# An attention tile's product with the carried state: q scaled ahead by GpSimd, and the sum made in one bank

## The chip, the cores and the metric

The kernel runs on one core of a Trainium2 chip. The metric is the device time of one execution in microseconds (us). PE is TensorE, DVE is VectorE, ACT is ScalarE, POOL is GpSimd and SP is the engine that issues the DMAs.

## The reference

Three stages follow each other. The first is an mLSTM attention with 2 batches, 8 heads, 768 steps and heads of 40; the second and third are two MoE layers (1536 tokens, width 320).

```python
for t in range(S):
    kt, vt, qt = (k[:, :, t], v[:, :, t], q[:, :, t])
    m_new = np.maximum(f_gate[:, :, t] + m, i_gate[:, :, t])
    f_stab = np.exp(f_gate[:, :, t] + m - m_new)
    i_stab = np.exp(i_gate[:, :, t] - m_new)
    m = m_new
    C = f_stab[:, :, None, None] * C + i_stab[:, :, None, None] * np.einsum('bhd,bhe->bhde', vt, kt)
    n = f_stab[:, :, None] * n + i_stab[:, :, None] * kt
    h_tilde = np.einsum('bhde,bhe->bhd', C, qt)
    nq = np.einsum('bhd,bhd->bh', n, qt)[:, :, None]
    denom = np.maximum(np.abs(nq), 1.0)
    o = 1.0 / (1.0 + np.exp(-o_gate[:, :, t]))
    y[:, :, t] = o * h_tilde / denom
```

Then `x = y`, `g(x @ w_in) @ w_out` with a piecewise g, and a second MoE of 8 experts whose gate weights are normalized eight times.

## The kernel before

**Attention.** The sequence is cut into chunks of 128 steps, and a tile is one chunk of one batch: 12 tiles, t = 2 * chunk + batch. Within a tile the recurrence is written as a masked product. `scores` (L434) multiplies keys by queries for four heads at a time into a bank of tag "at"; `scan` (L419) turns the gates f of the chunk, broadcast over the partitions by `load_g` (L171) into G0 or G1, into a triangle of decays on DVE; `gated` (L448) multiplies the scores by it into A; `values` (L425) and `keys` (L461) scale v and k on POOL; `values_sum` (L471) sums A by v in a bank "at". What earlier chunks left is the state `Cst`, one for each batch, 104 partitions by 4 pairs of heads by 82 columns: 40 rows and 41 columns for each head, two heads on the diagonal of a pair (the 41st column is n). `attn` (L523) multiplies q by the state into the bank "ax" (L540 to L542), scales the product by the decay since the chunk's start, which `gt` holds for each token in its columns 16 to 31 (L554), and adds the weighted sum to it (L558); both go through the tile `hv` on DVE. `gate_out` (L503) divides by the denominator and multiplies by the sigmoid into `sg`, `turn` (L513) transposes that into a bank "ax", and `split_x` (L140) writes it as two parts XH and XL. The state is multiplied by the whole chunk's decay on POOL (L550), `update` (L484) makes the new chunk's part in a bank "at", and `add_update` (L493) adds it to the state on DVE, in two instructions for the two heads of a pair (for the first chunk ACT copies it).

**Gates.** Before the tiles, `gate_max`, `gate_exps` and `gate_prods` (L363 to L393) make the gates in the rows g_f, g_i and g_m; g_m then holds the running products of f in each chunk. `gate_prods` writes g_f to DRAM (`g_d`), from where `load_g` broadcasts it. `gate_by_token` (L395) transposes g_i and g_m by 16 rows on PE into `gt`.

**Order.** Tiles 0 and 1 and the preparation of the first weights are written out by hand in one order (to L664, where `ordered` is cleared). From there tiles 2 to 11 are a generator of steps (`attn_rest`, L575), and the loop over the blocks of the first MoE (L787) takes `nf * RATE[si]` steps of it for each block (L838). Stage 0 makes the first half of the hidden units for tokens 0 to 511 in 8 blocks, stage 1 for tokens 512 to 1023 in 8 blocks; after stage 1 the rest of the attention is taken. In this part the framework's scheduler sets the order of each engine from its own estimate of the times, with the program's order as priority; each engine then runs its queue in order. PSUM banks come from `bank` (L94): two of tag "g1" for the MoE's first product, one each of "g2a", "g2b" and "g2c", two of "at", one of "ax". SP's DMAs (load_g, load_qk, load_kvo, and the loads of weight pieces) are one queue in order. The first tiles have warming matmuls (`warm`, L352) in the bank of the weighted sum.

The second MoE (from L1061) follows when the first is done.

Of the kernel before, what the change touches and what calls it, by code (L numbers as in the profile page):

```python
# [7 lines left out]
F32 = mybir.dt.float32  # L8
# [6 lines left out]
ALU = mybir.AluOpType  # L15
# [3 lines left out]
L = 128  # L19
# [15 lines left out]
WA, WG, WF = 4, 2, 12  # L35
RATE = (3.1, 4.5, 0, 0, 0)

# [6 lines left out]
def mlstm_moe_moe_kernel(  # L44
# [109 lines left out]
    with ExitStack() as atx:  # L154
# [10 lines left out]
        dram = ctx.enter_context(tc.tile_pool(name="dram", bufs=1, space=bass.MemoryType.DRAM))  # L165
        g_d = dram.tile([16, S - L], F32, name="g_d")
        nc.sync.dma_start(g_f, gates[:, S : 2 * S])
# [3 lines left out]
        def load_g(t):  # L171
            c, b = divmod(t, 2)
            nc.sync.dma_start(
                G1 if t % 2 else G0, g_d[b * 8 : b * 8 + 8, (c - 1) * L : c * L].unsqueeze(0).to_broadcast([128, 8, L])
            )

        def load_qk(t):
# [26 lines left out]
        for a in QK:  # L204
            vec.memset(a[32:64, 0:2], 0.0)
            vec.memset(a[64:128, 1], 0.0)
            gp.memset(a[0:64, 2], 0.0)


# [133 lines left out]
        lend = ap.tile([104, NCH * 8], F32, name="lend")  # L343
        gt = ap.tile([128, NCH, 32], F32, name="gt")
        Cst = ap.tile([104, B, 4, 82], F32, name="Cst")
# [30 lines left out]
        def gate_prods(c0, c1):  # L376
            if c0 == 0:
                act(out=g_s, in_=g_f[:, 0:L], func=ACTF.Copy)
            for c in range(c0, c1):
                cs = slice(c * L, (c + 1) * L)  # L380
                vec.tensor_tensor_scan(out=g_m[:, cs], data0=g_f[:, cs], data1=zer, initial=1.0, op0=ALU.mult, op1=ALU.add)
            if c0 == 0:
                vec.scalar_tensor_tensor(
                    out=g_s, in0=f(g_s), scalar=cst[0:32, C_N16 : C_N16 + 1], in1=g_f[:, 0:L], op0=ALU.mult, op1=ALU.add,
                )
                vec.tensor_copy(g_s[:, 0:1], zer[:, 0:1])
            else:
                gp.tensor_copy(
                    g_f[:, c0 * L : c1 * L].rearrange("p (c t) -> p c t", t=L)[:, :, 0:1], zer[:, 0 : c1 - c0].unsqueeze(2)
                )  # L390
                for j in range(4):
                    o = j // 2 * 8 + j % 2
                    nc.sync.dma_start(g_d[j * 4 : j * 4 + 4, :], g_f[o : o + 7 : 2, L:S])  # L393

        def gate_by_token(c0, c1):  # L395
            p = bank("g1")
            for c in range(c0, c1):
                cs = slice(c * L, (c + 1) * L)
                o = (c - c0) * 32
                transpose(p[:, o : o + 16], g_i[0:16, cs], ident[0:16, 0:16])  # L400
                transpose(p[:, o + 16 : o + 32], g_m[0:16, cs], ident[0:16, 0:16])
            act(out=gt[:, c0:c1, :], in_=p[:, 0 : 32 * (c1 - c0)].rearrange("p (c e) -> p c e", e=32), func=ACTF.Copy)

# [12 lines left out]

        scanned = set()

# [51 lines left out]

        def values_sum(A, vw, tag, n):  # L471
            pa = bank(tag)
            if n:
                warm(n, pa)
            for h in range(8):
                mm(pa[:, h * 41 : (h + 1) * 41], A[h % 2][:, h // 2, :], vw[:, h, :], start=True, stop=True)
            return pa
# [15 lines left out]
        def add_update(t, pu):  # L493
            c, b = divmod(t, 2)
            puv = pu[0:104, 0:328].rearrange("p (r d) -> p r d", r=4)
            for par in range(2):
                rs, es = slice(par * 64, par * 64 + 40), slice(par * 41, par * 41 + 41)
                if c:
                    vec.tensor_tensor(out=Cst[rs, b, :, es], in0=puv[rs, :, es], in1=Cst[rs, b, :, es], op=ALU.add)
                else:  # L500
                    act(out=Cst[rs, b, :, es], in_=puv[rs, :, es], func=ACTF.Copy)
# [18 lines left out]
        def heads(p):  # L520
            return p[:, 0:328].rearrange("p (h d) -> p h d", h=8)

        def attn(t):  # L523
            c, b = divmod(t, 2)
            last = c == NCH - 1
            if t not in scanned:
                scan(t)
            vw = values(t)
            yield
# [8 lines left out]
            if t + 2 < NTILE:  # L538
                load_g(t + 2)
            pi = bank("ax")  # L540
            for pr in range(4):
                mm(pi[:, pr * 82 : (pr + 1) * 82], tiles_in[t][0][0:104, 0, pr, :], Cst[:, b, pr, :], start=True, stop=True)  # L542
            pa = values_sum(A, vw, "at", WA if t < 5 else 0)
            if t + 1 < NTILE:
                scan(t + 1)
            sg = sigmoid(t)
            yield
            if not last:
# [4 lines left out]
                )  # L553
            hv = ap.tile([128, 8, 41], F32, name="hv", tag="hv")  # L554
            vec.tensor_tensor(
                out=hv, in0=heads(pi), in1=gt[:, c, 16 + b * 8 : 16 + b * 8 + 8].unsqueeze(2).to_broadcast([128, 8, 41]), op=ALU.mult,
            )
            vec.tensor_tensor(out=hv, in0=hv, in1=heads(pa), op=ALU.add)  # L558
            gate_out(hv, sg)
            yield  # L560
# [95 lines left out]
        for t in (2, 3):  # L656
            load_g(t)
        piece(2)
        piece(1)
# [622 lines left out]
```

## Time and profile before

| | us |
|---|---|
| median of 3 runs | 955.72 |
| lowest, highest | 955.15, 961.31 |
| the profiled execution's own time | 955.23 |
| its span, from first to last instruction | 952.2 |

The profile is of one execution, so sums are made against its own time. An engine's busy time counts its instructions; matmuls are pipelined, and the records show each until it has drained. Where a helper on line 69 records the operations, the names of the tiles tell them apart: `bk_at` is a bank of tag "at", and out<-in stands for what is written from what. A number in brackets is the idle time of the engine before the instruction and what released it.

### The profile page before, as it was taken

Reading aid. Unit: us, or ns where it says so; the run is one execution under the profiler, and the core shown is the slowest. Engines: PE = TensorE matmul, PEld = TensorE weight load, DVE = VectorE, ACT = ScalarE, POOL = GpSimd, SP = SyncE. Lnnn points to the kernel's source line nnn. Section 1 sums busy time; section 2 is a strip of 40 time slices with the busy share of each in tenths; the row PEclk is TensorE's granted clock in tenths of the full one; section 3 lists DMA queues with packets and bytes.
Section 4 is the critical chain, followed back from the end, with each engine's and each line's share of the span. In section 5 each row is a group of like instructions: output and inputs, shape, how many; then the busy total and the mean of one; then the engine's idle time right before and its main releaser. Section 6 shows DMA issues by size and latency. Waiting matters only on the chain.

```text
span 952.2 us, 14707 instructions
## 1 busy us (share of the span) xinstructions
PE 938.7 (99%) x5696; PEld 879.9 (92%) x5702; DVE 664.6 (70%) x1122; ACT 428.6 (45%) x766; POOL 310.3 (33%) x364
## 2 busy tenths in 40 slices
PE   9899999999999999999999999999999999999998
PEld 6689988878878899999999999999999999999998
DVE  8898884764553656767857866775786687678565
ACT  4764565978754333534414523432442443343211
POOL 3222210000017567674505612450461254144000
PEclk9999999999999999999999999999999999999999
DMA  8684530130011101201200210220120021010011
GB/s 250 197 229 138 171 113 2 34 116 2 1 45 40 34 5 45 67 23 59 73 15 23 73 50 1 62 78 6 30 87 28 8 84 55 1 48 26 1 43 42
DMA packets 36437, 57.22 MB, mean 60 GB/s; under 512 B 2976, under 2 KB 26400, under 8 KB 36368
## 3 DMA queue, kind: packets, MB, share of 16 engines
q1 hardware_dynamic: 36368, 56.29, 19.9%
q8 instruction: 44, 0.72, 0.3%
q14 instruction: 25, 0.20, 0.1%
HBM read 52.70 MB, written 2.01 MB: 57 GB/s over the span
## 4 chain that ended last, share of the span: by engine, by line
PE 89%; DVE 7%; ACT 2%; issue 1%; POOL 1%; DVEq 0%; POOLq 0%
PE bk_g L69 41%; PE bk_at L69 17%; PE bk_ax L69 9%; PE bk_g2c L69 8%; PE bk_g2a L69 7%; PE bk_g2b L69 7%; DVE g_all L69 1%; DVE G L69 1%; DVE raw L69 0%; DVE sg L69 0%; DVE wf L69 0%; DVE den L69 0%; DVE scr L69 0%; DVE wk L69 0%; DVE hv L69 0%
## 5 line engine op out<-in xcount | busy, mean ns | idle before, releaser
L69 ACT ACTIVATE hi<-t 128x768 fp32r<-128x768 f32 x112 | 94.8, 847 | 346.3 <-DVE t L69 346.3
L69 PE MATMUL bk_g<-XH,wk 128*128 128x512 f32 (+2 forms) x638 | 199.7, 365 | 2.3 <-DVE t L69 1.7
L69 DVE TENSOR_TENSOR t<-bk_g,t 128x384 f32<-128x384 f32 x224 | 124.4, 555 | 78.5 <-PE bk_g L69 76.6
L69 PE MATMUL bk_g<-XL,wk 128*128 128x512 f32 (+2 forms) x394 | 141.6, 360 | 0.0
L69 DVE SCALAR_TENSOR_TENSOR lo<-t,hi 128x768 fp32r<-128x768 f32 x112 | 117.1, 1045 | 29.1 <-ACT hi L69 29.1
L69 PEld LDWEIGHTS bk_g<-XH,wk 128*128 128x128 f32 x638 | 117.7, 188 | 17.2 <-DVE t L69 2.0
L960 POOL TENSOR_TENSOR cb<-cb 128x256 f32<-128x256 f32 (+1 forms) x136 | 103.1, 776 | 49.0 <-DMA cb<-in_w1q_dram 20.2
L69 PE MATMUL bk_at<-wf,hi 128*128 128x320 f32 x448 | 101.0, 308 | 0.0
L1101 POOL TENSOR_TENSOR acc<-acc,ev 128x320 f32<-128x320 f32 x36 | 43.4, 1236 | 154.8 <-ACT ev L69 154.7
L69 PEld LDWEIGHTS bk_g<-XL,wk 128*128 128x128 f32 x394 | 74.3, 189 | 6.9
L69 DVE TENSOR_TENSOR t<-bk_g,u 128x384 f32<-128x384 f32 x112 | 61.5, 549 | 25.1 <-PE bk_g L69 24.4
L69 PEld LDWEIGHTS bk_at<-wf,hi 128*128 128x128 f32 x448 | 78.2, 188 | 0.0
L69 PE MATMUL bk_g<-XH,wf 128*128 128x384 f32 x238 | 73.9, 339 | 0.0
L69 PE MATMUL bk_g2b<-wf,hi 128*128 128x320 f32 x272 | 70.8, 309 | 0.0
L69 PE MATMUL bk_ax<-wf,hi 128*128 128x320 f32 x272 | 70.6, 308 | 0.0
L69 PE MATMUL bk_at<-wf,lo 128*128 128x320 f32 x224 | 68.7, 307 | 0.0
L69 PE MATMUL bk_g2c<-wf,hi 128*128 128x320 f32 x272 | 62.0, 308 | 0.0
L69 PE MATMUL bk_g2a<-wf,hi 128*128 128x320 f32 x272 | 61.9, 308 | 0.0
L69 ACT ACTIVATE gs<-gs 128x512 f32<-128x512 f32 x96 | 60.4, 629 | 1.9
L967 POOL TENSOR_TENSOR wf<-cb,wf 64x256 fp32r<-64x256 f32 (+2 forms) x35 | 38.3, 1102 | 55.4 <-ACT wf L69 31.5
L69 DVE TENSOR_TENSOR gs<-bk_g,gs 128x512 f32<-128x512 f32 x40 | 27.6, 689 | 36.8 <-ACT gs L69 36.6
L1015 POOL TENSOR_TENSOR t<-XH,XL 128x384 f32<-128x384 f32 x3 | 3.0, 1011 | 153.0 <-DVE XL L69 153.0
(285 smaller groups left out, 2156.1 us busy)
## 6 DMA issues: line engine op xcount, KB each, us to landing
cb<-in_w1q_dram SPq DMA_DIRECT2D x28, 512.0 KB, 4.5
raw<-in_w_dram SPq DMA_DIRECT2D x32, 320.0 KB, 3.1
kvo_t<-in_kvo_dram SPq DMA_DIRECT2D x12, 484.0 KB, 4.1
raw<-in_w_out_dram SPq DMA_DIRECT2D x8, 639.5 KB, 10.0
raw<-in_w_in_dram SPq DMA_DIRECT2D x8, 511.8 KB, 7.0
qk<-in_qk_dram SPq DMA_DIRECT2D x24, 160.0 KB
G<-g_d SPq DMA_DIRECT2D x5, 512.0 KB, 4.3
g_all<-g_d SPq DMA_DIRECT2D x5, 512.0 KB, 3.6
```

Source lines behind the costliest of these rows:

```text
L69: r = fn(*args, **kw)
L960: gp.tensor_tensor(out=c[:, o], in0=c[:, x], in1=c[:, y], op=op)
L967: gp.tensor_tensor(out=u[64:128, :, 2], in0=x[64:128, :, 1], in1=f(u[64:128, :, 2]), op=ALU.subtract)
L1015: gp.tensor_tensor(out=c[:, o : o + 2], in0=f(xh[:, k]), in1=f(xl[:, k]), op=ALU.add)
L1101: gp.tensor_tensor(out=acc[:, t, :], in0=acc[:, t, :], in1=ev, op=ALU.add)
```

## The change

`dq` is a new tile: the decay of each step of the chunk, broadcast by DMA over the 40 rows of a head, which POOL multiplies by q in place. The product of dq and the state is summed in the bank of the weighted sum, so `hv` is gone and `gate_out` reads the bank. The decays go to DRAM from g_m (`d_d`), like g_f. `add_update` copies the bank to SBUF with ACT, and POOL adds. RATE for stage 1 goes from 4.5 to 5. The transposes of g_m for `gt` are gone. The rest of the diff is the two DQ buffers, their memsets, and `load_d(2)` and `load_d(3)` behind `load_g` of the same tiles.

```diff
-RATE = (3.1, 4.5, 0, 0, 0)
+RATE = (3.1, 5, 0, 0, 0)
...
+        def load_d(t):
+            c, b = divmod(t, 2)
+            for r in range(2):
+                nc.sync.dma_start(
+                    DQ[t % 2][r * 64 : r * 64 + 40],
+                    d_d[b * 8 + r * 4 : b * 8 + r * 4 + 4, (c - 1) * L : c * L].unsqueeze(0).to_broadcast([40, 4, L]),
+                )
...
+        DQ = [ap.tile([128, 4, 128], F32, name=f"dq{i}", tag=f"dq{i}", bufs=1) for i in range(2)]
+        for a in DQ:
+            gp.memset(a[32:64], 0.0)
...
+                for j in range(4):
+                    o = j // 2 * 8 + j % 2
+                    nc.sync.dma_start(d_d[j * 4 : j * 4 + 4, :], g_m[o : o + 7 : 2, L:S])
...
-                transpose(p[:, o + 16 : o + 32], g_m[0:16, cs], ident[0:16, 0:16])
...
+        def decayed(t):
+
+            dq = DQ[t % 2][0:104]
+            gp.tensor_tensor(out=dq, in0=dq, in1=tiles_in[t][0][0:104, 0], op=ALU.mult)
+            return dq
+
-        def values_sum(A, vw, tag, n):
+        def values_sum(A, vw, tag, n, state=None):
             pa = bank(tag)
             if n:
                 warm(n, pa)
+            if state is not None:
+                dq, b = state
+                for pr in range(4):
+                    mm(pa[:, pr * 82 : (pr + 1) * 82], dq[:, pr, :], Cst[:, b, pr, :], start=pr == 0, stop=False)
             for h in range(8):
-                mm(pa[:, h * 41 : (h + 1) * 41], A[h % 2][:, h // 2, :], vw[:, h, :], start=True, stop=True)
+                mm(pa[:, h * 41 : (h + 1) * 41], A[h % 2][:, h // 2, :], vw[:, h, :], start=state is None, stop=state is None or h == 7)
             return pa
...
             c, b = divmod(t, 2)
+            if c:
+                ue = ap.tile([104, 328], F32, name="ue", tag="ue")
+                act(out=ue, in_=pu[0:104, 0:328], func=ACTF.Copy)
+                pu = ue
             puv = pu[0:104, 0:328].rearrange("p (r d) -> p r d", r=4)
...
                 if c:
-                    vec.tensor_tensor(out=Cst[rs, b, :, es], in0=puv[rs, :, es], in1=Cst[rs, b, :, es], op=ALU.add)
+                    gp.tensor_tensor(out=Cst[rs, b, :, es], in0=puv[rs, :, es], in1=Cst[rs, b, :, es], op=ALU.add)
...
+            if t not in dqs:
+                dqs[t] = decayed(t)
             vw = values(t)
...
-            pi = bank("ax")
-            for pr in range(4):
-                mm(pi[:, pr * 82 : (pr + 1) * 82], tiles_in[t][0][0:104, 0, pr, :], Cst[:, b, pr, :], start=True, stop=True)
-            pa = values_sum(A, vw, "at", WA if t < 5 else 0)
+            pa = values_sum(A, vw, "at", WA if t < 5 else 0, (dqs.pop(t), b))
+            if t + 2 < NTILE:
+                load_d(t + 2)
             if t + 1 < NTILE:
                 scan(t + 1)
+                dqs[t + 1] = decayed(t + 1)
...
-            hv = ap.tile([128, 8, 41], F32, name="hv", tag="hv")
-            vec.tensor_tensor(
-                out=hv, in0=heads(pi), in1=gt[:, c, 16 + b * 8 : 16 + b * 8 + 8].unsqueeze(2).to_broadcast([128, 8, 41]), op=ALU.mult,
-            )
-            vec.tensor_tensor(out=hv, in0=hv, in1=heads(pa), op=ALU.add)
-            gate_out(hv, sg)
+            gate_out(heads(pa), sg)
```

## Rows read from the trace of the kernel before

**Rows 1.** The page's busy time of each engine, with its share and instructions.

```profile
PE 938.7 (99%) x5696; PEld 879.9 (92%) x5702; DVE 664.6 (70%) x1122; ACT 428.6 (45%) x766; POOL 310.3 (33%) x364
```

**Rows 2.** Busy time by stretches: PE, PEld, DVE, ACT, POOL, clock, DMA share, GB/s.

```profile
25.00:50.00 25.00, 21.77 (x158) 18.14 (x160) 20.29 (x32) 18.96 (x36) 6.41 (x8) 1.00 0.63 203
...
45.00:135.00 90.00, 86.20 (x665) 78.77 (x668) 80.67 (x150) 50.98 (x95) 21.82 (x25) 1.00 0.59 173
135.00:280.00 145.00, 145.00 (x662) 117.65 (x661) 81.18 (x134) 105.77 (x192) 0.00 (x0) 1.00 0.09 25
```

**Rows 3.** The chain of waits from 82 to 94 us, shares by line.

```profile
by line: DVE G L69 19.4%; issue 14.6%; DVE g_all L69 14.6%; DVE hv L69 11.6%; DVE A L69 9.9%; DVE sg L69 5.2%; DVE wf L69 5.2%; DVE bk_g L69 5.1%; DVE Cst L69 4.8%; DVE XL L69 4.7%; PE bk_ax L69 4.5%; ACT XH L69 4.2%; DVE den L69 2.8%
```

**Rows 4.** PE's waits from 45 to 135 us: us in total, times, longest.

```profile
PE bk_ax L69 <- DVE sg L69: 2.1, 3, 1.0
PE bk_at L69 <- DVE A L69: 0.9, 1, 0.9
PE bk_at L69 <- DVE Cst L69: 0.7, 2, 0.5
PE bk_at L69 <- DVE hv L69: 0.4, 1, 0.4
```

**Rows 5.** Timeline of DVE and of PE around 85 us: start, us, instruction.

```profile
84.88 0.31 DVE L69 TENSOR_TENSOR Cst<-bk_at,Cst 40x164 f32<-40x164 f32 x1
...
85.34 0.33 DVE L69 TENSOR_TENSOR Cst<-bk_at,Cst 40x164 f32<-40x164 f32 x1
85.70 0.52 DVE L69 TENSOR_TENSOR sg<-sg,den 128x320 f32<-128x320 f32 x1
...
85.03 0.40 PE L69 MATMUL bk_g<-XH,wk 128*128 128x256 f32 x2
86.37 0.53 PE L69 MATMUL bk_ax<-cst,sg 128*128 128x128 f32 x3 [0.94 <-DVE sg L69]
```

**Rows 6.** Groups by tile (hv, Cst, den): ns min/median/max, first and last start.

```profile
L69 DVE TENSOR_TENSOR hv<-bk_ax,gt x10: 468/492/501, 34.7 to 149.3; 128x328 f32<-128x328 f32 x10
L69 DVE TENSOR_TENSOR hv<-hv,bk_at x10: 465/488/497, 48.6 to 151.1; 128x328 f32<-128x328 f32 x10
...
L69 DVE TENSOR_TENSOR Cst<-bk_at,Cst x16: 306/326/332, 50.7 to 129.0; 40x164 f32<-40x164 f32 x16
...
L69 DVE TENSOR_SCALAR den<-bk_at x1: 155/155/155, 19.6 to 19.6; 128x8 f32<-128x8 f32 x1
```

**Rows 7.** Timeline of PE from 76 to 80 us.

```profile
76.25 1.96 PE L69 MATMUL bk_at<-qk 104*128 104x128 f32 x16
78.04 1.02 PE L69 MATMUL bk_ax<-Cst,qk 104*128 104x82 f32 x8
78.86 0.36 PE L69 MATMUL bk_g<-XL,wk 128*128 128x256 f32 x1
79.06 0.31 PE L69 MATMUL bk_at<-vw,A 128*128 128x41 f32 x2
```

**Rows 8.** Timeline of POOL and of DVE from 89 to 96 us.

```profile
89.86 0.73 POOL L550 TENSOR_TENSOR Cst<-Cst,lend 104x328 f32<-104x328 f32 x1 [3.99 <-PE bk_ax L69]
90.56 1.70 POOL L428 TENSOR_TENSOR vw<-kvo_t,gt 128x328 f32<-128x328 f32 x1
94.60 0.80 POOL L464 TENSOR_TENSOR kw<-kvo_t,g_all 128x320 f32<-128x320 f32 x1 [2.34 <-PE bk_at L69]
...
90.23 3.10 DVE L69 TENSOR_TENSOR_SCAN g_all<-g_all,id 128x512 f32<-128x512 f32 x2
...
94.72 0.70 DVE L69 TENSOR_TENSOR den<-hv,den 128x8 f32<-128x8 f32 x1
```

**Rows 9.** Groups of ACT, 28 to 135 us: busy, mean ns of one, idle before.

```profile
L69 ACT ACTIVATE XH<-bk_ax 128x384 fp32r<-128x384 f32 x8 | 3.9, 491 | 3.0 <-PE bk_ax L69 2.9
```

**Rows 10.** DMA issues on SP's queue, from the timeline.

```profile
25.46 2.51 SPq L393 DMA_DIRECT2D g_d<-g_all  x4
...
79.91 1.27 SPq L179 DMA_DIRECT2D qk<-in_qk_dram  x2
```

More of the change, by code (lines that the diff above doesn't have):

```diff
@@ L165, in mlstm_moe_moe_kernel @@
         dram = ctx.enter_context(tc.tile_pool(name="dram", bufs=1, space=bass.MemoryType.DRAM))
-        g_d = dram.tile([16, S - L], F32, name="g_d")
+        g_d, d_d = (dram.tile([16, S - L], F32, name=n) for n in ("g_d", "d_d"))
         nc.sync.dma_start(g_f, gates[:, S : 2 * S])
@@ L343, in mlstm_moe_moe_kernel @@
         lend = ap.tile([104, NCH * 8], F32, name="lend")
-        gt = ap.tile([128, NCH, 32], F32, name="gt")
+        gt = ap.tile([128, NCH, 16], F32, name="gt")
         Cst = ap.tile([104, B, 4, 82], F32, name="Cst")
@@ L398, in gate_by_token @@
                 cs = slice(c * L, (c + 1) * L)
-                o = (c - c0) * 32
+                o = (c - c0) * 16
                 transpose(p[:, o : o + 16], g_i[0:16, cs], ident[0:16, 0:16])
-                transpose(p[:, o + 16 : o + 32], g_m[0:16, cs], ident[0:16, 0:16])
-            act(out=gt[:, c0:c1, :], in_=p[:, 0 : 32 * (c1 - c0)].rearrange("p (c e) -> p c e", e=32), func=ACTF.Copy)
+            act(out=gt[:, c0:c1, :], in_=p[:, 0 : 16 * (c1 - c0)].rearrange("p (c e) -> p c e", e=16), func=ACTF.Copy)
         def gate_ends():
@@ L414, in gate_ends @@
             act(out=lend, in_=p[0:104, 0 : NCH * 8], func=ACTF.Copy)
-        scanned = set()
+        scanned, dqs = set(), {}
         def scan(t):
@@ L657, in mlstm_moe_moe_kernel @@
             load_g(t)
+        for t in (2, 3):
+            load_d(t)
         piece(2)
```

## The prediction

> **What bounds the kernel now.** First the page's busy times: PE is busy for 938.7 of 952.2 us [rows 1], so all that can be won without taking matmuls away is PE's idle time, 13.5 us by the records. The second view is the table by stretches. From 135 to 280 us PE has no idle time in the records at all; from 45 to 135 us, where most of the attention tiles 2 to 11 are woven into the first MoE, PE is busy for 86.20 of 90 and DVE for 80.67; from 25 to 50 us PE is busy for 21.77 of 25 [rows 2]. So in the stretch that the change touches DVE is nearly full, and PE idles 3.8 us by the records behind it. The third view is the chain of waits. Between 82 and 94 us most of it stands on DVE (G, g_all, hv, A, sg, Cst) [rows 3]: there DVE sets the pace, and from 135 us on PE does. The fourth view is PE's own waits from 45 to 135 us: 2.1 us on sg, which the turn to XH needs, 0.9 on A, 0.7 on the state's addition (whose bank the next scores want) and 0.4 on hv [rows 4], together 4.1 us. One such wait close up: PE's last matmuls begin at 85.03; DVE does the two state additions at 84.88 and 85.34, then the last product of sg at 85.70, and PE goes on at 86.37, with 0.94 us of idle time [rows 5]. Nothing outside 25 to 155 us is touched but a few early instructions, so the sum is one of PE's waits in this stretch.
>
> **The change part by part.**
>
> *DVE.* Two instructions on hv go in each of ten tiles: 10 x 0.492 + 10 x 0.488 = 9.8 us; two additions of 40x164 go in each of the eight tiles 2 to 9: 16 x 0.326 = 5.2 us [rows 6]. Together 15.0 us, some 1.6 us of a tile; the tiles follow each other by (149.3 - 34.7) / 9 = 12.7 us. What now reads the bank instead of hv costs the same: den from a bank took 155 ns in tile 0 [rows 6], where this path is already in use. So of DVE's 80.67 us in 90 some 15.0 x 90 / 127 = 10.6 go, 70 stay, and DVE has room. But 15.0 us is no gain of time: PE has real work beneath it, and only the waits of PE that hang on DVE can go.
>
> *PE.* The four state matmuls of a tile stay, with dq in q's place; they move from the bank of their own to the weighted sum's. The transposes of g_m that go are a few early ones of 16 columns; I count them at nothing. So PE's work is the same, and the sum is: the three waits on sg (2.1), of which the chain loses one hv instruction (0.49) and up to two additions (0.65), a little more than the 0.94 us that one of them lasts [rows 5, 6]: all 2.1 goes. The 0.7 on Cst goes, since a ScalarE copy frees that bank. Of the 0.4 on hv, half; of the 0.9 on A none, since A's instructions stay. That is 3.0 us. The records show a matmul as busy until it drains: eight small ones follow each other by 1.02 / 8 = 0.13 us [rows 7], so after the two at 85.03 PE could have gone on at 85.29, and the wait was 1.08 rather than 0.94 us [rows 5]: 0.14 more in each of some four waits, 0.6 us. Gain 3.6 us. What is late next is PE itself.
>
> *The state product loses its own bank.* Before, it could run while A was being made: scores at 76.25, product at 78.04, the weighted sum's first matmuls at 79.06 [rows 7]. Now it needs one of the two banks that the scores hold, and that is free only when DVE has multiplied the first A. What is queued behind it on PE is the weighted sum, the update, and then the next MoE matmuls as far as the schedule puts them behind. Cover: matmuls of bk_g and bk_g2c, which stand between in most tiles. Without cover it costs up to the time of the product, 8 records in (79.06 - 78.04) = 1.0 us at most, 0.9 without the drain, a tile; at best nothing. I take 0.4 us in all, near the lower end, because at 78.86 a matmul of bk_g was ready and ran.
>
> *GpSimd.* One product of 104x512 a tile. No such row is there; the 104x328 product took 0.73 us alone, and the 128x328 one 1.70 us when it stood against DVE [rows 8]. In proportion to the columns: 0.73 x 512/328 = 1.14 us, and at worst 2.65. The lower end is 0.73 itself. I take 1.14, ten times 11.4 us. Two additions of 40x164 in eight tiles: between DVE's 0.31 [rows 5] and the 0.73 of the product twice as wide; I take 0.4, so 16 x 0.4 = 6.4 us. POOL's load in 45 to 135 us goes from 21.82 [rows 2] to some 38 of 90 us: it isn't full. The new waits: dq(t+1) stands after the start of tile t and is wanted a tile later, and the state's additions are wanted two tiles later (a batch's state is used in every second tile), 11 us or more. Behind a waiting addition stand vw and kw of the next tile on POOL; PE waits for those only if they come later than A. I count the new waits at nothing; if the cover went, the price would be one addition and one product a tile, 1.9 us.
>
> *POOL against DVE.* The trace shows that they hold each other up: while vw ran on POOL from 90.56 for 1.70 us, the pair of scans at 90.23 took 3.10 us; the den instruction at 94.72 took 0.70 us beside kw at 94.60, where 155 ns is its size from a bank [rows 6, 8]. So a POOL instruction in the wrong place costs DVE some 0.70 - 0.155 = 0.55 us, and at most its own length. Three new ones a tile, of 1.14 + 2 x 0.4 = 1.9 us: from 0 to 1.9 us a tile. I take one hit, 0.6 us, which leaves DVE 1.0 us of the 1.6 that it was given; that suffices for the waits above.
> The Trainium skill, page "SBUF — State Buffer", section "Who interferes with whom", gives the rule for these rows: DVE and GpSimd share one port pair under an exclusive lock that is held for the whole instruction. By that rule the trace agrees (0.70 us for den beside 0.80 us of kw), and it speaks against the change: each product moved to GpSimd shuts out DVE instructions with two SBUF inputs, the scans first of all.
>
> *ScalarE.* Eight copies of 104x328 out of a bank: a 128x384 one takes 0.49 us [rows 9]; lower bound 0.4 by columns, upper 0.49: 3.6 us in 90, where ACT is busy for 50.98 [rows 2]. Nothing waits for it but the additions, and it frees the bank sooner. Count: nothing; if it delays a gs activation, 0.5 us a tile at most.
>
> *SP and DMA.* Four more writes to DRAM early (2.51 us for the four of g_d) and two broadcast loads a tile (two qk loads were issued in 1.27) [rows 10]. load_d(t+2) waits for the state matmuls of t, and the loads of qk and kvo queue behind it; these waited for the same matmuls before. Early, 2.51 + 4 x 0.64 = 5.1 us of issue stand ahead of some weight pieces. I count nothing; the bound is 5.1 us once. The early memsets of DQ on POOL lie beside the first loads. RATE (4.5 to 5) draws the last attention tiles closer together in the second stage, most of which is PE's alone [rows 2]: nothing, either way.
>
> **Sum.** The profiled execution took 955.23 us (span 952.2 and 3.0 around it), 0.5 below the median of 955.72. 955.23 - 3.6 + 0.4 = 952.0 us.
>
> **The rivals.**
> *Hidden anyway (H).* PE was the bound after all: the scheduler orders the instructions anew, and other waits take the place of those that go. For it: a PE that is busy for 96% of the stretch already [rows 2]. Against it: three waits on one and the same cause. 954 to 957 us, say 955.2.
> *The bank (B), the other side.* The state product waits for A in each tile without cover: 0.9 x 10 = 9.0 us, less the 3.6: 960.6. It decides against the kernel from 0.36 us a tile upwards. For it: PE's wait of 0.9 us on A [rows 4] is just such a place, and tiles 2 to 4 put warming matmuls in the same bank first. Against it: close up, another matmul stood ready [rows 7].
> *The lock (L).* All three POOL instructions hit DVE: 1.9 us a tile against the 1.6 taken away. DVE is where it was or 0.3 us a tile worse, 955.2 + 10 x 0.3 = 958.2. For it: each scan pair needs both inputs from SBUF, and took 3.10 us beside POOL [rows 8]. Against it: POOL would run them in the pauses in which it waits now (3.99 us before 89.86) [rows 8].
> This is the outcome that the rule of the Trainium skill's page "SBUF — State Buffer" would have if every new POOL instruction met a DVE instruction with two SBUF inputs.
> *More than the waits (M).* DVE sets the pace more widely than the records say, and PE's hidden drains and the idle time of 25 to 50 us (3.2) go too: 3.6 + 3.2 + 2 = 8.8, so 946.4.
>
> **How the numbers follow.** Forecast (950 to 954) 0.44; H 0.24; B 0.14; L 0.10; M 0.08. A difference of about 1% (9.6 us, 946.2 or 965.3) is what a measurement of this kernel can tell from no change. Faster by that much: most of it from M, 0.06; slower: B with the queue's 5.1 us on top (965.7), 0.06; within: 0.88. The range takes in M's 946.4 and B's 960.6, with a little of the early queue: 946.0 to 961.0.
>
> **What would show it.** Right: hv and DVE's Cst gone; PE's waits on sg and Cst between 45 and 135 us below 1 us in sum; PE's busy share there above 97%; DVE's busy time there 70 to 75 us; the product on POOL 1.1 to 1.3 us; the stretch to the end of the attention shorter by some 4 us, all after it the same length. Wrong: PE waiting on dq or on A before the state matmuls (B); scan pairs near 3 us as a rule and den near 0.7 (L); matmuls of a later stage that take another time.

## The result, and the profile after

The changed kernel takes 965.0 us (median of 9 runs, 962.35 to 969.67); the kernel before, on the same chip, 955.15 (9 runs). The ratio is 1.0096, with a 95% interval of 1.0076 to 1.0116: 9 us slower, about the 1% that the prediction took as its limit, where 952.0 was forecast and 961.0 was the upper end of the range. The profiled execution took 965.0 us, its span is 963.0, 10.8 more than before.

First the page's busy times, to be read beside [rows 1].

```profile
PE 945.2 (98%) x5696; PEld 885.0 (92%) x5696; DVE 656.9 (68%) x1086; ACT 430.7 (45%) x774; POOL 339.6 (35%) x392
```

PE has six matmuls fewer than before (the transposes; PEld counts 5702 and 5696, and in PE's own count of before six records are missing), but is busy 6.5 us longer, and idle for 963.0 - 945.2 = 17.8 us instead of 13.5. So the 10.8 us have two parts: 4.3 of idle time, 6.5 of matmuls that last longer. DVE is busy 7.7 us less, though instructions worth 15.0 us went. The same stretches as in [rows 2], in the view by stretches:

```profile
25.00:50.00 25.00, 21.43 (x138) 16.75 (x136) 20.67 (x31) 16.47 (x33) 7.42 (x8) 0.93 0.66 207
45.00:135.00 90.00, 83.52 (x641) 75.47 (x640) 69.72 (x108) 47.38 (x91) 46.18 (x46) 0.98 0.58 163
135.00:280.00 145.00, 143.75 (x664) 116.85 (x663) 82.70 (x137) 108.82 (x199) 6.07 (x6) 1.00 0.15 45
```

From 45 to 135 us DVE is busy for 69.72 of 90, where it was 80.67, and yet PE does less: 83.52 instead of 86.20. POOL has doubled, 46.18 instead of 21.82. And the seventh number, the granted clock, is no longer 1.00. PE's waits in that stretch, beside [rows 4]:

```profile
PE bk_ax L69 <- DVE sg L69: 1.5, 1, 1.5
PE bk_at L69 <- DVE A L69: 1.2, 1, 1.2
PE bk_ax L69 <- ACT held L69: 0.7, 1, 0.7
PE bk_g L69 <- ACT XH L69: 0.6, 1, 0.6
PE bk_at L69 <- POOL kw L476: 0.5, 1, 0.5
PE bk_at L69 <- POOL dq L486: 0.4, 1, 0.4
```

The waits on Cst and hv are gone, as forecast, and sg is down by 0.6; but there are new ones on ACT and POOL, and these six, the largest of eleven, come to 4.9 us where the four of before, all that it has there, were 4.1. Two of them, on held and on XH, lie together around 113 us, where the second stage of the MoE begins. Microsecond by microsecond:

```profile
112.00:113.00 1.00, 0.27 (x3) 0.20 (x2) 0.64 (x3) 1.00 (x3) 0.59 (x1) 1.00 0.62 155
113.00:114.00 1.00, 0.56 (x3) 0.14 (x1) 0.00 (x0) 0.58 (x3) 0.86 (x3) 1.00 1.04 267
114.00:115.00 1.00, 0.65 (x3) 0.35 (x3) 0.56 (x1) 0.66 (x2) 1.00 (x2) 1.00 0.94 266
115.00:116.00 1.00, 1.00 (x4) 0.79 (x4) 0.00 (x0) 0.00 (x0) 1.00 (x3) 0.59 0.97 355
116.00:117.00 1.00, 1.00 (x5) 0.91 (x5) 0.00 (x0) 0.00 (x0) 0.41 (x1) 0.50 0.94 376
117.00:118.00 1.00, 1.00 (x7) 1.00 (x6) 0.00 (x0) 0.00 (x0) 0.00 (x0) 0.50 0.12 45
118.00:119.00 1.00, 1.00 (x5) 0.82 (x5) 0.69 (x1) 0.00 (x0) 0.00 (x0) 0.70 0.00 0
```

PE works 1.48 of 3 us, because the first stage's MoE matmuls are used up and the next need tile 7's XH. Then its clock is granted at 0.50, that is 1.2 GHz instead of 2.4, for some 3.4 us, and it does 0.41 + 0.50 + 0.50 + 0.30 = 1.7 us less work in that time. The profile of the kernel before shows 1.00 throughout; that after shows four such falls (from 16.4, 29.9, 115.4 and 398.2 us). Three stand behind a stretch in which PE was not full; ahead of the one at 16.4 the records have PE busy without a pause from 7.7 us on. Four times 1.7 is 6.8 us, about the 6.5 by which the matmuls last longer. No sentence of the prediction speaks of the clock.

A profile is one execution, though, and the falls come and go from one to the next. The nine runs of after have mean granted clocks from 0.985 (969.67 us) to 0.998 (963.33 us). Those of the kernel before that were run beside the experiments, 81 of them, go from 1.000 (26 runs, median 954.3 us) to 0.991 (7 runs, 960.0 to 962.5). So the kernel before falls too, only more seldom. In its one run at 0.998 after is still 9 us slower than before; at 0.992 against before's 0.991 it is 4 us slower (965.0 against 960.8 in the median).

### The profile page after: what moved, and what is told of

The parts are those of the page before. It is cut to its first block, busy times and chain, and to the rows that moved or that the text cites. A ratio compares the mean times of both kernels' runs of the same rounds, so it can differ in the third digit from the quotient of the medians.

```text
span 963.0 us, 14765 instructions
## 1 busy us (share of the span) xinstructions
PE 945.2 (98%) x5696; PEld 885.0 (92%) x5696; DVE 656.9 (68%) x1086; ACT 430.7 (45%) x774; POOL 339.6 (35%) x392
## 4 chain that ended last, share of the span: by engine, by line
PE 91%; DVE 4%; DMA 1%; ACT 1%; issue 1%; POOL 0%; SPq 0%; DVEq 0%; ACTq 0%; POOLq 0%
PE bk_g L69 41%; PE bk_at L69 19%; PE bk_ax L69 8%; PE bk_g2c L69 8%; PE bk_g2a L69 8%; PE bk_g2b L69 7%; DMA raw<-in_w_in_dram 1%; DVE g_all L69 1%; DVE sg L69 1%; DVE raw L69 0%; DVE wf L69 0%; ACT wf L69 0%; DVE qk L69 0%; DVE acc L69 0%; DVE wk L69 0%
## 5 line engine op out<-in xcount | busy, mean ns | idle before, releaser
L69 PE MATMUL bk_g<-XL,wf 128*128 128x384 f32 x154 | 52.5, 341 | 0.0
```

What stands on the lines that cost most here:

```text
L69: r = fn(*args, **kw)
```

## The experiments

The expectations below use letters for theories; each says what its own letters mean. Ratios are to the kernel before, run on the same chip beside each set of kernels (954.74 to 955.31 us). Some kernels leave out part of the computation: q is not in the product in e5 and e13, the decay is not in it in e9 and e17.

### Is it GpSimd's product?

```diff
-            gp.tensor_tensor(out=dq, in0=dq, in1=tiles_in[t][0][0:104, 0], op=ALU.mult)
```

> The changed kernel without GpSimd's product of the decay and q: the state is multiplied by the decay alone (the factor q is left out). Loads, bank and additions stay. If the product is what holds VectorE up (theory L, 1.52 us each beside scans of 4.16 and sg of 1.56 us), TensorE's waits on sg from 20 to 165 us fall from 2.7 to under 1 us, and the time from 965 to 959 or below. If the bank of the weighted sum is the cause (theory B), it stays within 2 us of 965. If the loads on SP's queue are (theory Q), it stays too.

958.38 us, ratio 1.0024 (1.0006 to 1.0041). With the product the ratio is 1.0096, so it costs some 0.7% or 6.9 us, give or take 2.5; the forecast had it at nothing on the path. PE's waits on sg from 20 to 165 us fall from 2.7 to 1.9 us, not below 1 as theory L has it. The groups of after, from 28 to 165 us, say how (busy time, mean ns of one, idle time before):

```profile
L486 POOL TENSOR_TENSOR dq<-dq,qk 104x512 f32<-104x512 f32 x10 | 15.2, 1520 | 1.1 <-DMA qk<-in_qk_dram 0.5
L69 DVE TENSOR_TENSOR_SCAN g_all<-g_all,id 128x512 f32<-128x512 f32 x10 | 14.9, 1519 | 0.0
L69 DVE TENSOR_TENSOR_SCAN G<-G,id 128x512 f32<-128x512 f32 x10 | 13.0, 1337 | 0.0
L525 POOL TENSOR_TENSOR Cst<-ue,Cst 40x164 f32<-40x164 f32 x16 | 12.7, 792 | 16.9 <-ACT ue L69 16.4
...
L69 DVE TENSOR_TENSOR sg<-sg,den 128x320 f32<-128x320 f32 x10 | 7.6, 763 | 0.2
```

The same view of before:

```profile
L69 DVE TENSOR_TENSOR_SCAN g_all<-g_all,id 128x512 f32<-128x512 f32 x10 | 12.5, 1287 | 0.0
L69 DVE TENSOR_TENSOR_SCAN G<-G,id 128x512 f32<-128x512 f32 x10 | 11.7, 1206 | 0.0
...
L69 DVE TENSOR_TENSOR sg<-sg,den 128x320 f32<-128x320 f32 x10 | 4.9, 489 | 0.2
```

One product takes 1.52 us in the mean, not 1.14. DVE's scans and sg last 3.7 + 2.7 = 6.4 us longer than before, which is most of the 7.3 us that DVE did not get of its 15.0. In e5, without the product, the three groups take 12.2, 13.0 and 6.7 us: 3.6 of the 6.4 us go with the product, 2.8 stay with GpSimd's additions. One place close up:

```profile
136.91 1.61 POOL L486 TENSOR_TENSOR dq<-dq,qk 104x512 f32<-104x512 f32 x1
137.31 1.56 DVE L69 TENSOR_TENSOR sg<-sg,den 128x320 f32<-128x320 f32 x1
...
139.01 0.41 PE L69 MATMUL bk_ax<-cst,sg 128*128 128x128 f32 x2 [1.21 <-DVE sg L69]
```

sg, 0.49 us when alone, takes 1.56 and ends 0.35 us behind the product, and PE waits 1.21 us for it. The Trainium skill, page "SBUF — State Buffer", section "Who interferes with whom", has an exclusive lock on a shared port pair here; by that rule the trace agrees (1.56 us beside 1.61).

The product alone, put on the kernel before (a copy of it into a tile that nothing reads):

```diff
                 scan(t + 1)
+                product(t + 1)
...
+        def product(t):
+            q = tiles_in[t][0][0:104, 0]
+            gp.tensor_tensor(out=spare, in0=q, in1=q, op=ALU.mult)
```

> Kernel before with one more GpSimd instruction in nine tiles, a product of 104x512 by 104x512 of the next tile's q into a tile of its own that nothing reads, behind the next tile's scan as in the changed kernel. Theory L (GpSimd's product holds VectorE up, whatever the bank and hv): 958 to 962 us, with VectorE's scans above 1.3 and 1.25 us and TensorE's waits on sg above the 2.1 us of before. Theory N (the price comes from the chain through dq and the merged bank, not from the product's running): 955 to 956 us.

957.85 us, ratio 1.0031 (1.0007 to 1.0055): about 3 us, at the lower edge of what was expected. The place of [rows 8] shows the rise, the pair of scans from 3.10 to 4.05 us:

```profile
91.14 4.05 DVE L69 TENSOR_TENSOR_SCAN g_all<-g_all,id 128x512 f32<-128x512 f32 x2
91.46 1.04 POOL L475 TENSOR_TENSOR spare<-qk 104x512 f32<-104x512 f32 x1
92.46 1.65 POOL L428 TENSOR_TENSOR vw<-kvo_t,gt 128x328 f32<-128x328 f32 x1
```

PE's waits on sg from 20 to 165 us are 3.1 us, where before had 2.1. So the product holds DVE up without the bank, hv or the loads; but that is 3 of some 7 us, so not all of its price.

Moving the product to DVE takes its part of the lock away (the additions stay on GpSimd):

```diff
-            gp.tensor_tensor(out=dq, in0=dq, in1=tiles_in[t][0][0:104, 0], op=ALU.mult)
+            vec.tensor_tensor(out=dq, in0=dq, in1=tiles_in[t][0][0:104, 0], op=ALU.mult)
```

> The changed kernel with the product of the decay and q on VectorE, 0.7 us each, ten times. Theory L: the 7 us that VectorE gets cost less than the lock took, and the time falls to 959 to 962. Theory B and theory C: within 2 us of 965 or above, since VectorE has 7 us more to do.

964.36 us, ratio 1.0094 (1.0064 to 1.0125): as slow as after, where theory L had 959 to 962. Here PE stands still for dq itself, at the first woven tile, and its clock is low for 10 us behind it (50.3 to 60.7 us):

```profile
PE bk_at L69 <- DVE dq L69: 2.1, 1, 2.1
```

The engine was not the whole matter, then.

### Is it the additions, RATE, or the bank?

The additions back on DVE, out of the bank:

```diff
-            if c:
-                ue = ap.tile([104, 328], F32, name="ue", tag="ue")
-                act(out=ue, in_=pu[0:104, 0:328], func=ACTF.Copy)
-                pu = ue
...
-                    gp.tensor_tensor(out=Cst[rs, b, :, es], in0=puv[rs, :, es], in1=Cst[rs, b, :, es], op=ALU.add)
+                    vec.tensor_tensor(out=Cst[rs, b, :, es], in0=puv[rs, :, es], in1=Cst[rs, b, :, es], op=ALU.add)
```

> The changed kernel with the state's additions back on VectorE from the bank (no ScalarE copy). If GpSimd's additions, 0.79 us each in the mean and in VectorE's way, are what costs (theory L), about 16 x 0.4 to 0.8 us of lost time goes and the time falls from 965 by 4 to 7 us, to 958 to 961, and the scans of g_all fall from 1.52 to under 1.4 us in the mean. If the slower clock of TensorE in three stretches is the cause (theory C), the falls at 16 and 30 us stay and the time stays within 2 us of 965. If the bank of the weighted sum is (theory B), it stays at 965 or rises, since VectorE has more to do again.

965.33 us, ratio 1.0114 (1.0086 to 1.0142): no gain, though GpSimd has 12.7 us less to do. PE's waits from 20 to 165 us are 3.7 us on sg and 1.3 on Cst, where after has 2.7 and none: the additions are DVE's own work again. The reverse, the copy and POOL's additions alone on the kernel before:

> The kernel before with the state's additions alone moved: ScalarE copies the bank, GpSimd adds. Theory L: slower than before by 3 to 6 us (958 to 961), scans and other VectorE instructions with two SBUF inputs longer. Theory C and theory B: within 1.5 us of 955, since neither the start nor the bank of the state product is touched.

957.95 us, ratio 1.0032 (1.0008 to 1.0056): slower by about 3 us, with 4.1 us of waits on sg in that stretch. The additions on POOL take 0.72 us each there and 0.79 after, twice the 0.4 that was forecast.

RATE back to 4.5 in the kernel after, and 5 alone in the kernel before:

```diff
-RATE = (3.1, 5, 0, 0, 0)
+RATE = (3.1, 4.5, 0, 0, 0)
```

> The changed kernel with RATE back at 4.5. If the pace at which the attention is taken in the second stage is part of the loss (theory R), 3 us or more come back, to 962 or below. By L and C it is within 2 us of 965, since 5 of the 8.6 us are lost before the second stage begins.

> Kernel before with RATE 5 in place of 4.5 and nothing else. If RATE is worth nothing, 955 us within 1; if it is a part of the loss, 957 or more; if it was what the change could have given, 953 or less.

964.42 us (1.0059 to 1.0129) and 956.1 us, ratio 1.0006 (0.9981 to 1.0031): RATE is worth nothing that can be measured, as forecast.

The state product back in its own bank, so that it no longer waits for the scores' bank; ScalarE brings it to hv and one DVE addition joins the two:

```diff
-            pa = values_sum(A, vw, "at", WA if t < 5 else 0, (dqs.pop(t), b))
+            pi = bank("ax")
+            dq = dqs.pop(t)
+            for pr in range(4):
+                mm(pi[:, pr * 82 : (pr + 1) * 82], dq[:, pr, :], Cst[:, b, pr, :], start=True, stop=True)
+            pa = values_sum(A, vw, "at", WA if t < 5 else 0)
...
-            gate_out(heads(pa), sg)
+            hv = ap.tile([128, 8, 41], F32, name="hv", tag="hv")
+            act(out=hv, in_=heads(pi), func=ACTF.Copy)
+            vec.tensor_tensor(out=hv, in0=hv, in1=heads(pa), op=ALU.add)
+            gate_out(hv, sg)
```

> The changed kernel with the state product back in the bank of its own, ax; ScalarE copies it to hv and VectorE adds the weighted sum to it. Theory B (the product waits until the first A has freed a bank): the bank back gives 3 us or more, in spite of 0.49 us a tile on VectorE, to 962 or below. Theory L: the additions are back on VectorE's way to sg, the time stays at 965 or rises by up to 4 us.

970.3 us, ratio 1.0153 (1.0132 to 1.0174). With the bank back the kernel is 5 us slower, where theory B had it 3 us faster. The edit is not of the bank alone: it also brings ten copies on ScalarE and ten additions on DVE, and PE has a new wait of 4.0 us on wf. That the merged bank, the prediction's rival B, is not the cause rests on e9 below, which keeps it and is faster than the kernel before.

### The clock

The memsets of DQ stood behind the memset of qk in POOL's queue, and PE waits 0.45 us for g_s at 7.7 us, ahead of the fall at 16.4 us. They go behind the memset of Cst:

```diff
-        for a in DQ:
-            gp.memset(a[32:64], 0.0)
...
         gp.memset(Cst, 0.0)
+        for a in DQ:
+            gp.memset(a[32:64], 0.0)
```

> The changed kernel with GpSimd's two memsets of DQ moved behind its other memsets. Theory C: they delay the first scans by some 0.4 us, TensorE waits 0.45 us at 7.7 us and its clock is halved from 16.4 to 19.5 us; without them that fall goes, and 1 to 2 us come back (963 to 964). Theory L: the stretch is not part of it, the time stays within 0.5 us of 965.

963.04 us, ratio 1.0082 (1.0065 to 1.0099). The step from after is 2 us by the medians, and the intervals overlap. The profiled execution, the fastest of the four (961.3 us, mean clock 0.998), has no wait on g_s, and its clock at 16 and at 30 us is whole:

```profile
16.00:20.00 4.00, 3.84 (x26) 2.54 (x25) 3.76 (x6) 3.97 (x6) 0.74 (x1) 1.00 1.02 295
30.00:34.00 4.00, 3.59 (x28) 3.08 (x27) 3.00 (x4) 3.88 (x10) 2.36 (x3) 1.00 0.56 161
```

The other three runs have 0.992 to 0.994, about what after has. And e14 below, with the same late memsets, waits 0.27 us for g_s and falls at 16 us all the same:

```profile
16.00:20.00 4.00, 4.00 (x19) 2.79 (x18) 3.09 (x4) 3.95 (x6) 0.74 (x1) 0.57 1.04 254
```

The last instruction on g_s starts at 7.27 us in both; what differs is that PE's nine warming matmuls ahead of it last 3.30 us in e2 and 2.91 in e14. e7, with the early memsets, waits 0.65 us and does not fall there. That the memsets cause the fall is not shown.

Nor does the idle time around 113 us bring the fall by itself. In e2's profile PE has the same waits there (0.72 us on held, 0.58 on XH) and works 1.50 of 3 us, and the clock stays whole behind them:

```profile
110.00:113.00 3.00, 1.50 (x11) 0.89 (x9) 1.28 (x7) 2.13 (x6) 1.82 (x3) 1.00 0.72 184
```

On top of that, more warming matmuls at the start (2 before the first `gate_rows`, 7 before `gate_ends`):

> The changed kernel with the memsets late as in e2, and with warming matmuls (two before 7.4 us, seven before the gate ends at 27 us) where TensorE idles in the start. Theory C: the falls of the clock at 16 and 30 us go in all runs; each halves the clock for 3.3 us and costs up to 1.65 us; against e2 (963.0) another 0 to 1.7 us come back, and the mean granted clock is 0.996 or above. If the falls are not caused by those idle times, the time stays at 963.

963.22 us, ratio 1.0078 (1.0057 to 1.0098): nothing beyond e2, and two of the four runs have a mean clock of 0.994. And RATE 3.5 for the first stage, against PE running dry at 112 us:

```diff
-RATE = (3.1, 5, 0, 0, 0)
+RATE = (3.5, 5, 0, 0, 0)
```

> Kernel after with the late memsets (963.0 alone) and RATE 3.5 in place of 3.1 in the first stage, so that the first stage's MoE work is spread over more attention tiles. If TensorE's idle time at 112 to 115 us, where the next MoE block has to wait for the tile's XH, and the half clock behind it cost what they seem to (0.7 + 0.6 us of waits and 1.65 us of clock), 960 to 961 us; if the late VectorE merely shows at another place, 963 or more.

965.02 us, ratio 1.0097 (1.0067 to 1.0127): a miss. PE waits for the same XH (0.58 us at 115.29), and has a new wait of 3.3 us on wf.

### The chain from before to after, edit by edit

Everything that only dq needs is taken out: the writes and loads of the decays, the memsets, the product; q stands in its place, and the additions are on DVE.

```diff
             dq = DQ[t % 2][0:104]
-            gp.tensor_tensor(out=dq, in0=dq, in1=tiles_in[t][0][0:104, 0], op=ALU.mult)
-            return dq
+            return tiles_in[t][0][0:104, 0]
...
-            if t + 2 < NTILE:
-                load_d(t + 2)
...
-                for j in range(4):
-                    o = j // 2 * 8 + j % 2
-                    nc.sync.dma_start(d_d[j * 4 : j * 4 + 4, :], g_m[o : o + 7 : 2, L:S])
```

> Kernel after with q itself in the place of dq (the decay is left out of the state's share): no loads of the decay, no memsets of DQ, no product, and the state's additions back on VectorE out of the bank. What is left of the change is the state product in the weighted sum's bank, the missing hv instructions, the smaller transposes and RATE. Theory C (what costs is what was put on GpSimd and on the queue; the merged bank gives a little): 951 to 954 us, below the kernel before. Theory B (the merged bank costs and what goes from VectorE is worth nothing): 957 to 960 us, as without the product alone (958.4).

951.28 us, ratio 0.9958 (0.9938 to 0.9977): faster than before. This is the part of the change that the prediction's gain comes from, but for the additions, which stay on DVE. Of PE's 4.1 us of waits from 45 to 135 us one row is left, and PE is busy for 88.88 of the 90 us:

```profile
PE bk_at L69 <- DVE A L69: 1.0, 3, 0.4
```

(A wait of 1.18 us on A stands just ahead of that stretch, at 44.51; before has the like of it, 0.90 us, at 45.28.)

```profile
45.00:135.00 90.00, 88.88 (x699) 81.77 (x698) 76.05 (x140) 50.67 (x97) 21.27 (x25) 1.00 0.60 173
```

Then the writes alone are put back, and writes and loads with the memsets in their late place (there dq is the decay by itself):

> The kernel without the q chain (951.3) with the four writes of the decays to DRAM put back, and nothing else: no loads of them, no memsets, no product; q stands in the place of dq. Between that kernel and the one with writes, loads and memsets (962.0) lie 10.7 us. Theory Q1 (the early place in SP's queue: the writes take 2.4 us there, the first loads of G and of weight pieces come later by as much): 954 to 957 us. Theory Q2 (the loads, four at the start and two a tile, and the order that the framework's scheduler makes with them): 951 to 952.5 us.

> Kernel after without the product, as in the earlier run of that name (958.4), but with the state's additions on VectorE and the memsets of DQ behind that of Cst: the writes and loads of the decay are what stands between it and the kernel without the whole q chain (951.3). If the writes and loads cost nothing, 951 to 953 us, and the 7 us between those two runs were the memsets and GpSimd's additions; if they cost, 954 to 957.

954.1 us, ratio 0.9993 (0.9978 to 1.0008), and 962.03 us, ratio 1.0054 (1.0033 to 1.0076). e17 falls on Q1; e13 is dearer than either side expected. So the writes and the loads, with the matmuls reading the loaded tile in place of q, cost 0.96%, 9 us, by e9 and e13. By e5, which has the same DMAs, and GpSimd's additions and the early memsets as well (ratio 1.0024), it is 0.66% or 6 us. The two differ mostly in the clock: e5's runs have 0.995 to 0.998, e13's 0.992 to 0.998. Runs at one mean granted clock, 0.998, can be set side by side:

| runs at 0.998 | us |
|---|---|
| before, 15 runs, median | 954.5 |
| e9, 2 runs | 951.4, 951.7 |
| e17 (writes), 5 runs, median | 954.0 |
| e5 (writes, loads, additions on POOL, early memsets), 5 runs, median | 958.4 |
| e13 (writes, loads), 1 run | 958.8 |
| e3, e2, e8 (the whole change; RATE, memsets, warming differ), 1 run each | 960.2, 961.3, 961.5 |
| after, 1 run | 963.3 |

So the DMAs cost some 7 us with the clock nearly whole too (from one run of e13 and five of e5). SP's queue, in e9, then with the writes alone, then with the loads:

```profile
29.79 0.51 SPq L226 DMA_DIRECT2D raw<-in_w_in_dram  x1
```


```profile
27.95 2.39 SPq L403 DMA_DIRECT2D d_d<-g_all  x4
30.44 0.39 SPq L173 DMA_DIRECT2D G<-g_d  x1
30.93 0.52 SPq L226 DMA_DIRECT2D raw<-in_w_in_dram  x1
```

```profile
31.80 0.56 SPq L173 DMA_DIRECT2D G<-g_d  x1
32.41 0.52 SPq L180 DMA_DIRECT2D dq<-d_d  x1
33.17 0.39 SPq L173 DMA_DIRECT2D g_all<-g_d  x1
33.60 1.92 SPq L180 DMA_DIRECT2D dq<-d_d  x3
35.62 0.36 SPq L227 DMA_DIRECT2D raw<-in_w_in_dram  x1
```

The first of these weight pieces is issued at 29.79 us in e9, at 30.93 in e17 and at 35.62 in e13. Later PE's queue itself is in another order. The 16 matmuls of tile 5's scores, and the first 512-wide matmul of the second stage, in the timeline of PE of e17 and then of e13:

```profile
74.54 1.95 PE L69 MATMUL bk_at<-qk 104*128 104x128 f32 x16
...
107.18 0.50 PE L69 MATMUL bk_g<-XH,wk 128*128 128x512 f32 x1
```

```profile
81.27 1.95 PE L69 MATMUL bk_at<-qk 104*128 104x128 f32 x16
...
111.63 0.73 PE L69 MATMUL bk_g<-XH,wk 128*128 128x512 f32 x2 [0.58 <-ACT XH L69]
```

With the loads tile 5's scores come 6.7 us later, although its q and k were issued at 57.02 us and PE hardly idles in between: MoE matmuls stand ahead of them in PE's queue. These are missing at the end of the first stage, when tile 7 is late and PE has nothing else. From 100 to 120 us, in the view by stretches, e17 and then e13:

```profile
100.00:120.00 20.00, 19.43 (x145) 17.61 (x144) 15.92 (x29) 11.56 (x23) 7.12 (x8) 1.00 0.68 224
```

```profile
100.00:120.00 20.00, 17.77 (x129) 16.35 (x127) 13.65 (x23) 7.89 (x16) 7.44 (x7) 0.91 0.47 146
```

PE idles 1.7 us longer there in e13, and the half clock takes another 1.7: 3.4 of the 5.0 us by which its span is longer than e17's. After has 18.45 there, at 0.91; before:

```profile
100.00:120.00 20.00, 19.99 (x151) 18.25 (x150) 17.19 (x32) 11.43 (x20) 6.72 (x8) 1.00 0.66 206
```

The last two edits of the chain are the product on POOL (e14) and the additions on POOL (e2, above):

> Kernel after with the additions on VectorE and the late memsets: of the GpSimd work of the change only the product is left, and the whole computation is done. The parts taken singly (951.3 without the q chain, 6.6 for the product, 0 to 2 for the loads) say 958 to 960 us; if the product alone carries the loss, 961 or more; 956 or less if the product was dear only together with the additions.

967.49 us, ratio 1.0116 (1.0068 to 1.0163): slower than expected, and slower than after by the medians (the intervals overlap). Its four runs have mean clocks of 0.984 to 0.992, so part of this step may be the clock.

| step | ratio to before | that step, in us of 955 |
|---|---|---|
| merged bank, no hv, smaller transposes, RATE (e9) | 0.9958 | -4.0 |
| writes of the decays (e17) | 0.9993 | +3.3 |
| loads, late memsets (e13) | 1.0054 | +5.8 |
| product on POOL (e14) | 1.0116 | +5.9 |
| additions on POOL (e2) | 1.0082 | -3.2 |
| early memsets (after) | 1.0096 | +1.3 |

The intervals of the ratios make the first three steps sure to about 2.5 us each and the fourth to 5; the last two can't be told from nothing. e9 and e17 leave out the decay, e13 leaves out q. The steps hold in this order alone: POOL's additions cost 3 us on the kernel before and seem to give 3 here, the product 3 us there and 6 or 7 here.

### A version with the whole computation that is faster?

If the product's place is what matters, it should go to DVE behind the second scores' multiplication, where DVE waits for the weighted sum (the expectation's 2.2 us "in each tile" is too much: after has 7.5 us of such waits, in four of the ten tiles). Additions on DVE, late memsets; in e15 and e16 the writes of the decays also stand behind the loads of G.

```diff
-                dqs[t + 1] = decayed(t + 1)
...
                 A.append(gated(t, hf, p))
                 yield
+            if t == 2:
+                dqs[t] = decayed(t)
+            if t + 1 < NTILE:
+                dqs[t + 1] = decayed(t + 1)
```

> As the run before, with the product on VectorE, placed behind the multiplication of the second scores, where VectorE waits some 2.2 us for the weighted sum in each tile, and with the writes and loads of the decay behind the loads of G. The whole computation is done. If the loss is a matter of where and on which engine the product stands (theory L), its 0.65 us lie in that pause and the time is 951 to 954 us, at or below the kernel before; if VectorE has no room for it (theory V: as many instructions as before, other names), 955 to 958.

> As the run before, with the product on GpSimd in the same place of the program. GpSimd is not held by VectorE's order, so it runs the product as soon as its own queue and the loads let it, earlier than VectorE's pause. Theory L: between the run before and the one with the product in its old place, 955 to 958 us; if order on GpSimd alone was the trouble, as good as the run before.

> The whole computation: kernel after with additions on VectorE, late memsets, and the product on VectorE behind the multiplication of the second scores, as in the earlier run of that kind (965.9), but with the writes of the decays in their old place: there they stood behind the loads of G and waited 5.6 us for one of them. If that wait, and the first load of the decay behind it, was what kept that run slow: 956 to 959 us. If it is the loads and the order as such, 962 or more, and no version with the q chain comes near the kernel before.

965.88 us, ratio 1.0108 (1.0078 to 1.0137), 973.37 (1.0130 to 1.0254) and 963.8 (1.0061 to 1.0147). The first two miss; e18 falls on its second alternative, the loads and the order as such. In e15 the moved writes were themselves late, since G1 lies in the same tile as the decays that are written, and dq's loads behind them:

```profile
SPq L180 <- DVE dq L69: 8.6, 1, 8.6
SPq L677 <- DMA g_all<-g_d: 5.6, 1, 5.6
```

e18, without that wait, is within the interval of e15, and there PE waits 2.1 us for dq, as in e6. No version with the chain of dq came below the kernel before.

## Why the prediction was wrong

*The steps that failed* are two. The first is "SP and DMA": "I count nothing; the bound is 5.1 us once". The writes and loads cost 0.96% or 9 us by e9 and e13, 6 to 7 us by e5 and at an equal clock, where no product ran. The early part was seen and left out of the sum (weight pieces came 6 us later). The other part wasn't thought of: with these transfers the order of PE's queue is another, tiles 4 and 5 come later, and most of the price is paid at the end of the stage, not where the load stands. That the order is another with the loads is shown by e17 against e13 (which also has the memsets, late); why the scheduler orders so was not tried, and no run has the loads with PE's old order.

*GpSimd and the lock* is the second: "I take one hit, 0.6 us, which leaves DVE 1.0 us" was too little, and the product, counted at nothing on the path, costs some 7 us (e5). The product takes 1.52 us instead of 1.14, an addition 0.79 instead of 0.4, and DVE's scans and sg alone lost 6.4 us of the 15.0. The prediction's own sign of L came: a pair of scans takes 1.52 + 1.34 = 2.86 us in the mean. POOL's load was off as well: 21.82 + (11.4 + 6.4) x 90 / 127 is 34 of 90 us, not "some 38", and 46.18 was measured. Yet rival L as it was priced (1.9 us a tile against 1.6) would have made 958.2; e12 with its 3 us beside e5 with 7 puts the product beside DVE at about half of its price, roughly, since each figure is sure to about 2.5 us (nine products there, 1.04 us in the median; both their inputs are one tile). What the other half is stays open: the longer product, dq as an input of PE's chain, or the clock.
The Trainium skill, page "GPSIMD Engine Reference", section "Elementwise — side-by-side cycle accounting", has a two-input operation take about twice as long there as on VectorE. The trace agrees: the median product of 104x512 is 1.30 us on POOL, DVE's multiplication of 128x512 into A 0.69; the estimate by columns from a smaller POOL product was too short.

*PE's waits and the bank* were right in kind and in their sum, the sum in part by luck. 3.6 gained and 0.4 given back made 952.0; e9 took 951.28, its span is 3.2 us shorter than before's, and the waits on sg, Cst and hv are gone from its trace. But the additions, which the forecast moved away for part of that gain, still stand on DVE in e9, and PE's waits on A from 20 to 165 us go from 0.9 to 2.2 us: 1.3 us more where the bank was to take 0.4. DVE's busy time from 45 to 135 us, forecast at 70, is 69.72 in after. That DVE has room is no gain where something else is late. B is wrong: e9 has the merged bank and is faster than before, and e7 without it is slower still.

*What the sum left out* is the clock: 6.5 of the 10.8 us in the profiled execution. A wait of PE was priced at its length. Around 113 us PE idled 1.5 us and then lost 1.7 more. That is not the clock's part of the loss in general: at a mean clock of 0.998 the kernels with the whole change are still 6 to 9 us above the kernel before (four runs), so the greater part is lost without it. What decides whether the clock falls behind a given wait stays open. "Early memsets lie beside the first loads" is not shown to fail: after waits 0.45 us for g_s, e14 with late memsets 0.27.

*ScalarE and RATE.* RATE at nothing holds: e3 and e10 show no effect. A ue copy takes 0.44 us (forecast 0.4 to 0.49), but "Nothing waits for it but the additions" does not hold in after: in ACT's queue the copy at 111.83 us, which had waited for PE, stands ahead of held, and PE waits 0.73 us for held. The traces without the copies (e1, e13, e14) do not have that wait; how much of it is the copy's is not shown.

The range ended at 961.0 since each bound was added alone. The writes' 5.1 us were kept for the rival B; added to L they would have made 963.3, inside what was measured. That would have been near by luck, for the lock is about half of the product's price and the loads cost more than their issue.

## What to carry to other kernels

Price a DMA added to a full queue by what stands behind it, and then follow that to the next point where two streams of work meet: here the weight pieces were late at 36 us, tile 5 at 81, and the loss came at 110, where PE ran out of the one stream and waited for the other. Relieving an engine that is off the path is worth only the waits that hang on it (some 3 to 4 us, where 15.0 us of instructions were to go); whatever the relief needs elsewhere, a shared port, a queue, a place in the order, is paid in full. And measure such a change by parts in both directions, since its parts don't add up.

## What was not expected of the hardware

PE's granted clock fell to 0.50 behind stretches in which PE still did half of its work (1.48 of 3 us), and stayed there for 3.4 us; in e6, behind a wait of 2.1 us, for 10. The like stretch does not always bring a fall: e2 has 1.50 of 3 us without one, and e3 and e13 wait 2.2 and 2.1 us near 393 us, as after does at 397.9, with the clock at 1.00. The falls are not in every run of a kernel, so the times scatter: after from 962.35 to 969.67, before from 953.4 to 962.5. GpSimd's addition of 40x164 takes 0.54 us at the least, more than half as long as its product of 104x328 (0.73), which has twice the columns: the small ones don't come in proportion.
